# Limiting the upper words of 15 weight tiles in one ScalarE step, with a new early order on every engine

## The chip, the cores and the metric

The kernel runs on one core of one Trainium2 chip. The metric is the device time of one execution in microseconds; lower is better. The five engines of the core take part: TensorE (PE, with its weight loads as PEld), VectorE (DVE), ScalarE (ACT), GpSimd (POOL) and SyncE (SP), which here does nothing but issue DMAs.

## What is computed

Two layers, one after the other. The first is a gated linear attention over 4 batches, 8 heads, 768 positions and a head size of 48; the second takes its output as 3072 tokens of 384 values through a gated pair of matrix products with a hidden size of 2048.

```python
f = 1.0 / (1.0 + np.exp(-f_logit))
for t in range(S):
    state = f[:, :, t, :, None] * state + np.einsum('bhd,bhe->bhde', k[:, :, t], v[:, :, t])
    y[:, :, t] = np.einsum('bhd,bhde->bhe', q[:, :, t], state)
...
h = x @ w_in
relu6 = np.clip(h + 3.0, 0.0, 6.0)
g = h * relu6 / 6.0
return (g @ w_out).astype(np.float32)
```

The weights `w_in` and `w_out` come as float64 and are turned into float32 on the chip.

## The kernel before

**Units and groups.** The attention is cut into 24 units (`UNITS`): 6 blocks of 128 positions by 4 batches. Four units of one block make a group of 512 tokens, and each group then goes through 16 tiles `f` of 128 hidden columns: `mm1.f` (9 products of 128x128 with 128x512: high and low parts of weights and tokens, three of the four pairings), `relu.f` and `gh.f` on ACT, `g.f` and `gl.f` on DVE or POOL, `mm2.f` (9 products again). So 96 steps of each kind fill the program; `mm1.3` is tile 3 of group 0, `mm1.17` tile 1 of group 1. Tiles 0 to 2 of group 0 are computed in two halves of 256 tokens, `mm1a`/`mm2a` on units 0 and 1 and `mm1b`/`mm2b` on units 2 and 3, so that PE can begin when two units are done.

**One unit** `i` goes through: `load`, `loadq`, `loadv` (DMA of the gates, of q and k, of v), `gate` (sigmoid, ACT), `back` (a scan, DVE), `rend`, `end` (small), `kmul` (DVE or POOL), `fwd` (a scan, DVE), `qmul` (DVE or POOL); then on PE `tk` (transposes, copied out by `ktok` on ACT), `kv` (added up by `carry0` and `carry1`), `att` (masked by `mask` on DVE), `qs` and `av`; then `xh` (ACT) and `xl` write the high and the low part of the unit's output into `xts`. `xl` is a subtraction on DVE, or, where the order has `ym` for that unit, two products with minus the identity on PE and a copy on ACT. `hole` is two DMAs of 48 KB inside `xts`, which put rows where the next products expect them; `mm1a` waits for `hole.0` and `hole.1`, `mm1b` for `hole.2` and `hole.3`. In before, all of them are issued by SP.

**One weight tile** `f` goes through: `ld` (768 KB by DMA, issued by SP), the limit of the upper 16-bit words into `y`, `z` (ACT, L279: the lower words), `mid` (DVE, L286), `dif` (DVE, L291), `top` (DVE, L295: joins the two), `high` (ACT, L307: the high part as float32r) and `low` (DVE or POOL, L310: the rest). For tiles 0 to 2 half of `low` is split off: `wd` is a DMA, `lowi` the first half. The limit has two forms: for nine tiles (`ON_ACT`) ACT does two steps, `cy` (L267) and `lim` (L271), and for the other seven (0, 3, 7, 8, 13, 14, 15) DVE does one step, `lim` (L273).

**The order.** `ORDER` is a list of such tokens, made by a planner outside of the program. Each engine runs its own instructions in exactly the order in which the list names them (L844 to L849), and waits where an operand isn't there. `ON_POOL` names the steps that POOL does in DVE's place. `warm.N` and `tiny.N` are products of a blank tile that no one reads: they keep PE at work while it has nothing else. SP's list is in order too: a DMA whose buffer is still in use holds back all that stand behind it. DMAs share 8 semaphores in turn, so that one can also wait for the eighth before it.

Of the kernel before, what the change touches and what calls it, by code (L numbers as in the profile page):

```python
# [46 lines left out]
kmul.1 kmul.3 lowi.0 lowi.1 kmul.4 decay.4 kmul.5 qmul.5 decay.5 kmul.6 gl.4 decay.6 gl.5 qmul.6 kmul.7 low.10 low.11  # L47
gl.11 kmul.8 gl.14 qmul.9 lowo.0 kmul.9 decay.8 qmul.10 kmul.10 decay.9 decay.10 lowo.2 kmul.12 decay.12 qmul.13
qmul.14 qmul.15 kmul.15 decay.15 qmul.16 decay.16 qmul.17 qmul.18 decay.18 kmul.20 decay.19 decay.21 kmul.21 decay.22
kmul.22 qmul.23  # L50
# [6 lines left out]
end.0 warm.1 ktok.0 qmul.0 kv.0.0 back.1 load.2 att.0.2 carry0.0 ld.1 warm.1 loadq.2 rend.1 kmul.1 mask.0 fwd.1 tk.1.4
qs.0.0 lim.0 av.0 qmul.1 gate.2 warm.2 end.1 mid.0 ktok.1 load.3 back.2 loadq.3 carry1.0 kv.1.2 xh.0 loadv.2 z.0 ld.2
warm.9 rend.2 dif.0 loadv.3 fwd.2 cy.1 lim.1 top.0 ym.0 att.1.2 mid.1 gate.3 kmul.2 carry1.1 end.2 qmul.2 xl.0 tk.2.4
warm.2 carry0.1 mask.1 high.0 wd.0 qs.1.0 back.3 av.1 loadq.4 hole.0 att.2.2 xh.1 dif.1 kmul.3 warm.4 z.1 xl.1 load.4  # L60
mask.2 ktok.2 hole.1 lowi.0 cy.2 rend.3 top.1 tk.3.4 warm.2 ld.3 kv.2.2 ktok.3 lim.2 kv.3.0 fwd.3 carry0.2 z.2 warm.2
mid.2 qs.2.2 qmul.3 warm.2 carry1.3 dif.2 load.5 att.3.0 gate.4 ld.4 top.2 av.2 high.1 wd.1 mm1a.0.4 loadv.4 carry0.3
mask.3 lowi.1 end.3 carry1.2 loadq.5 xh.2 back.4 warm.1 high.2 ym.2 qs.3.0 relua.0 av.3 lowi.2 xl.2 kmul.4 lim.3
warm.1 xh.3 hole.2 mm1a.1.2 ga.0 end.4 xl.3 mm2a.0 relua.1 hole.3 decay.4 gate.5 ga.1 mid.3 z.3 rend.4 mm1a.2.1 dif.3
ld.5 fwd.4 wd.2 cy.4 ld.6 tk.4.4 mm2a.1 loadq.6 lim.4 qmul.4 top.3 ktok.4 ld.7 z.4 att.4.2 load.6 mid.4 ld.8 mm1b.0.4
back.5 relua.2 ld.9 high.3 ld.14 mm1b.1.0 ga.2 kmul.5 relub.0 rend.5 gb.0 cy.5 dif.4 kv.4.2 ld.10 mm1b.2.1 low.3 lim.5
loadv.5 top.4 mm2b.0 z.5 carry0.4 relub.1 mid.5 mm2a.2 mask.4 high.4 gb.1 cy.6 carry1.4 dif.5 mm2b.1 low.4 relub.2
lim.6 top.5 tk.5.0 mm1.3.3 z.6 mid.6 fwd.5 mm1.4.4 dif.6 qmul.5 relu.3 gb.2 end.5 high.5 g.3 decay.5 gate.6 low.5
att.5.2 ktok.5 mm2b.2 relu.4 back.6 top.6 qs.4.0 kmul.6 av.4 loadq.7 g.4 high.6 loadv.6 mask.5 loadv.7 mm1.5.4 gh.3
ld.12 lim.7 gh.4 load.7 low.6 ld.11 xh.4 gl.4 ld.15 gl.3 mm2.3 relu.5 rend.6 z.7 g.5 mid.7 z.8 lim.8 mm2.4 dif.7 gh.5  # L70
top.7 z.9 mid.8 mm1.6.2 high.7 dif.8 cy.9 low.7 end.6 top.8 kv.5.0 decay.6 relu.6 tk.6.4 lim.9 mm1.7.3 carry0.5 xl.4
gl.5 cy.10 mid.9 high.8 fwd.6 qs.5.0 relu.7 av.5 dif.9 qmul.6 mm2.5 xh.5 loadv.8 carry1.5 g.7 loadq.8 ktok.6 g.6 z.10
low.8 ym.5 lim.10 mm1.8.4 top.9 gate.7 gh.6 back.7 high.9 att.6.2 mid.10 gh.7 kv.6.0 kmul.7 gl.6 mm2.6 cy.11 rend.7
mask.6 lim.11 dif.10 z.11 low.9 tk.7.2 mm1.9.3 top.10 ktok.7 relu.8 fwd.7 high.10 end.7 relu.9 low.10 gl.7 mm2.7 g.8
carry0.6 gh.8 mm1.10.4 g.9 cy.12 carry1.6 qmul.7 xl.5 mid.11 load.9 gl.8 lim.12 mm2.8 ld.13 decay.7 hole.5 dif.11 gh.9
mid.12 z.12 dif.12 qs.6.2 top.11 att.7.0 loadq.9 top.12 av.6 high.11 load.8 kv.7.0 relu.10 gl.9 mm2.9 low.11 xh.6
carry0.7 mask.7 z.14 g.10 gate.9 qs.7.0 xl.6 z.13 lim.13 av.7 hole.6 mid.13 mm1.11.2 xh.7 lim.14 gh.10 loadv.9 dif.13
hole.4 mid.14 high.12 gl.10 mm2.10 top.13 relu.11 gate.8 g.11 low.12 gh.11 mm1.12.3 high.13 gl.11 carry1.7 xl.7 low.13
hole.7 mm1.13.4 dif.14 loadq.10 top.14 mm2.11 back.8 high.14 relu.12 low.14 kmul.8 z.15 mm1.14.1 lim.15 relu.13 g.12
g.13 mid.15 mm1.16.0 gh.13 dif.15 top.15 gl.13 tk.8.2 high.15 mm2.13 end.8 gh.12 low.15 relu.14 rend.8 gl.12 mm1.15.4  # L80
fwd.8 qmul.8 mm2.12 back.9 relu.15 load.10 relu.16 g.15 ktok.8 g.14 att.8.2 g.16 kv.8.2 gh.14 mm1.17.4 mask.8 gl.14
rend.9 gate.10 fwd.9 gh.15 mm2.14 gl.15 qmul.9 back.10 mm2.15 lowo.0 mm1.19.1 outs.0 outv.1 kmul.9 end.9 gh.16 outs.2
gl.16 decay.8 relu.17 mm1.18.0 od.2 rend.10 load.11 relu.19 g.17 od.0 carry0.8 fwd.10 mm2.16 relu.18 g.19 end.10
qmul.10 carry1.8 g.18 tk.9.3 kmul.10 load.12 lowo.1 mm1.20.4 loadv.10 ktok.9 od.1 gh.17 decay.9 gh.18 gl.17 gate.11
qs.8.0 back.11 att.9.2 decay.10 loadq.11 av.8 kv.9.2 gl.18 xh.8 mm2.17 gate.12 carry0.9 carry1.9 lowo.2 end.11 mask.9
mm1.21.2 gh.19 gl.19 xl.8 tk.10.3 relu.21 mm2.18 ktok.10 g.21 relu.20 rend.11 back.12 qs.9.0 gh.21 fwd.11 att.10.2
loadq.12 av.9 kv.10.0 qmul.11 mm2.19 g.20 load.13 loadv.11 carry0.10 gl.21 loadv.12 carry1.10 mm1.22.4 rend.12 fwd.12
kmul.12 mask.10 mm2.21 relu.22 g.22 decay.11 gh.22 kmul.11 mm1.23.3 gate.13 qmul.12 xh.9 back.13 load.14 hole.8
tk.11.4 relu.23 gl.22 mm2.22 ktok.11 xl.9 gh.20 g.23 hole.9 gl.20 qs.10.0 rend.13 att.11.2 gate.14 loadq.13 av.10
kv.11.0 loadv.13 tk.12.4 mm2.20 ktok.12 gh.23 end.12 gl.23 decay.12 mm1.24.4 mask.11 kmul.13 mm1.25.3 mm2.23 relu.25  # L90
relu.24 g.25 g.24 mm1.29.3 gh.24 gl.24 fwd.13 mm1.26.4 relu.29 gh.25 qmul.13 xh.10 gl.25 mm2.25 load.15 xl.10 relu.26
carry0.11 back.14 mm2.24 g.29 g.26 qs.11.0 gh.26 att.12.2 gl.26 av.11 kv.12.2 loadv.14 xh.11 carry1.11 mm2.26 mask.12
hole.10 gh.29 carry0.12 gate.15 carry1.12 loadq.14 rend.14 mm1.27.4 tk.13.2 relu.27 mm1.30.3 g.27 gl.29 xl.11 mm2.29
relu.30 hole.11 gh.27 g.30 end.13 kmul.14 mm1.28.1 gl.27 gh.30 ktok.13 gl.30 decay.13 back.15 tk.14.0 mm2.30 fwd.14
qmul.14 mm1.31.2 load.16 mm1.32.4 relu.31 relu.28 g.31 end.14 g.28 mm2.27 relu.32 ktok.14 qs.12.0 gh.28 att.13.2 gh.31
loadq.15 gl.28 av.12 kv.13.2 g.32 xh.12 mm2.28 decay.14 gate.16 mask.13 rend.15 carry0.13 carry1.13 fwd.15 mm1.33.4
# [870 lines left out]
```

## Time and profile before

| | |
|---|---|
| device time, median of 3 runs | 466.39 us (466.26 to 467.24) |
| span of the profiled execution | 464.7 us |
| PE busy | 453.4 us, 98% of the span |
| DVE, ACT, POOL busy | 291.0, 212.4, 64.3 us |
| DMA | 44.91 MB |

The profiled execution is told by its span, from its first to its last instruction; the page has no other time of it. The median of the timed runs is 1.7 us above the span, and that is what lies around it. PE's busy time counts the blank products too, and overlapping instructions once; the idle time of an engine is what stands "before" its instructions, with the event that ended it. Where two instructions of one engine follow each other without a wait, the second starts some 0.1 us before the first one's end, so that sums over a queue go by start to start.

### The profile page before, as it was taken

The numbers are of one execution on the slowest core, as the hardware profiler recorded it, in microseconds if no ns is written. First come the engines' busy times: TensorE is split into PE (matmuls) and PEld (weight loads), VectorE is DVE, ScalarE is ACT, GpSimd is POOL, SyncE is SP. The second block draws the span as 40 slices with busy tenths as digits, with TensorE's granted clock in tenths as the row PEclk, the third lists the DMA queues.
The fourth block names the chain that finished last, engine by engine and source line by source line (L and its number), as shares of the span: only waits on it lengthen the run. The fifth ranks groups of instructions, "written<-read, shape, count | busy, mean of one in ns | idle before, by whom it ended". The sixth has DMA issues, their size and how long they took to land.

```text
span 464.7 us, 11482 instructions
## 1 busy us (share of the span) xinstructions
PE 453.4 (98%) x4967; PEld 386.6 (83%) x4967; DVE 291.0 (63%) x455; ACT 212.4 (46%) x365; POOL 64.3 (14%) x65
## 2 busy tenths in 40 slices
...
GB/s 302 306 294 335 360 242 24 204 54 26 176 108 104 24 81 59 132 74 84 82 0 1 110 75 155 56 57 2 95 1 20 8 1 0 2 135 1 0 1 74
DMA packets 19113, 44.91 MB, mean 97 GB/s; under 512 B 2544, under 2 KB 8816, under 8 KB 19056
## 3 DMA queue, kind: packets, MB, share of 16 engines
...
q10 hardware_dynamic: 288, 0.26, 0.2%
q14 instruction: 16, 0.13, 0.1%
...
## 4 chain that ended last, share of the span: by engine, by line
PE 90%; DVE 3%; DMA 2%; ACT 2%; issue 1%; SPq 0%; POOL 0%; POOLq 0%
PE o L643 35%; PE pair L599 26%; PE single L599 11%; PE pair L514 3%; PE pair L444 2%; DMA v<-unit 2%; PE pair L531 2%; PE o L684 2%; PE idle L822 2%; PE pair L482 2%; PE pair L699 1%; PE single L699 1%; PE pair L463 1%; PE pair L665 1%; ACT w L279 1%
## 5 line engine op out<-in xcount | busy, mean ns | idle before, releaser
L643 PE MATMUL o<-gg,weight 128*128 128x512 f32 x705 | 165.7, 382 | 0.4 <-DVE gg L626 0.3
L643 PEld LDWEIGHTS o<-gg,weight 128*128 128x128 f32 x705 | 131.1, 189 | 19.8 <-DVE gg L626 1.6
L599 PE MATMUL pair<-xts,weight 128*128 128x512 f32 x576 | 133.1, 381 | 0.0
L599 PEld LDWEIGHTS pair<-xts,weight 128*128 128x128 f32 x576 | 107.6, 189 | 15.1 <-DVE tg L613 0.3
L626 DVE TENSOR_TENSOR gg<-tg,gg 128x512 fp32r<-128x512 f32 x75 | 56.0, 751 | 55.6 <-ACT gg L622 55.4
L622 ACT ACTIVATE gg<-tg 128x512 fp32r<-128x512 f32 x79 | 48.9, 626 | 65.7 <-PE o L643 51.3
L613 DVE SCALAR_TENSOR_TENSOR tg<-tg,pair 128x512 f32<-128x512 f32 x64 | 43.4, 683 | 55.8 <-ACT tg L609 55.6
L609 ACT ACTIVATE tg<-pair,half 128x512 f32<-128x512 f32 x64 | 43.5, 684 | 72.4 <-PE pair L599 69.1
L599 PE MATMUL single<-xts,weight 128*128 128x512 f32 x261 | 61.9, 382 | 0.0
L599 PEld LDWEIGHTS single<-xts,weight 128*128 128x128 f32 x261 | 48.5, 189 | 7.0 <-DVE tg L613 0.2
L609 ACT ACTIVATE tg<-single,half 128x512 f32<-128x512 f32 x29 | 19.9, 685 | 32.8 <-PE single L599 29.2
L376 DVE TENSOR_TENSOR_SCAN suffix<-gates,unit 112x516 f32<-112x516 f32 (+1 forms) x25 | 29.4, 1180 | 4.2 <-ACT gates L369 4.2
L400 DVE TENSOR_TENSOR_SCAN gates<-gates,rend 112x516 f32<-112x516 f32 x24 | 30.4, 1266 | 0.3
L389 POOL TENSOR_TENSOR qkf<-qkf,suffix 112x512 f32<-112x512 f32 x14 | 21.1, 1507 | 64.7 <-DVE suffix L376 22.2
L613 DVE SCALAR_TENSOR_TENSOR tg<-tg,single 128x512 f32<-128x512 f32 x29 | 19.8, 682 | 9.9 <-ACT tg L609 9.6
L408 POOL TENSOR_TENSOR decayed<-state,ends 112x192 f32<-112x192 f32 x13 | 10.6, 819 | 109.8 <-PE pair L514 65.8
L405 POOL TENSOR_TENSOR qkf<-qkf,gates 112x512 f32<-112x512 f32 x11 | 15.8, 1437 | 67.0 <-DVE gates L400 39.3
L550 ACT ACTIVATE xts<-pair 112x512 fp32r<-112x512 f32 x24 | 14.2, 594 | 23.6 <-PE pair L531 19.0
L451 DVE TENSOR_TENSOR a<-pair,causal 128x512 f32<-128x512 f32 x24 | 16.4, 683 | 8.2 <-PE pair L482 5.3
L643 PE MATMUL o<-xts,weight 128*128 128x512 f32 x84 | 20.3, 380 | 0.0
L563 DVE TENSOR_TENSOR xts<-pair,xts 112x512 fp32r<-112x512 f32 x21 | 14.4, 684 | 7.6 <-ACT xts L550 7.6
L626 DVE TENSOR_TENSOR xts<-tg,xts 128x512 fp32r<-128x512 f32 x14 | 9.5, 690 | 13.9 <-ACT xts L622 13.9
...
## 6 DMA issues: line engine op xcount, KB each, us to landing
...
```

The source lines that it names most:

```text
L376: nc.vector.tensor_tensor_scan(flat(sf[:, p])[:, ::-1], gt[:, columns(p)][:, ::-1], flat(unit[:, p])[:, ::-1], 0.0, op0=ALU.mult, op1=ALU.add,
L389: engine("kmul", i).tensor_tensor(parts_of(t, 1), parts_of(t, 1), split(sf[:, :, 1:C + 1]), op=ALU.mult)
L400: nc.vector.tensor_tensor_scan(past, past, flat(rend), 0.0, op0=ALU.mult, op1=ALU.add)
L405: engine("qmul", i).tensor_tensor(parts_of(t, 0), parts_of(t, 0), split(to), op=ALU.mult)
L451: nc.vector.tensor_tensor(d["a"].rearrange("r p e t -> r e p t"), d["at"], causal.unsqueeze(1).unsqueeze(1).broadcast_to([128, 2, NP, HC]) ...
L563: nc.vector.tensor_tensor(parts(1), d["y"][:PR], parts(0).bitcast(F32), op=ALU.subtract)
L599: nc.tensor.matmul(h, win(f, a, k), turned(g["xt"][:, k, :g["n"] // C, b]), start=i == 0, stop=i == 3 * KT - 1,)
L609: nc.scalar.activation(d["t"], d["h"], AF.Relu, bias=half, scale=1.0 / 6.0)
L613: nc.vector.scalar_tensor_tensor(d["t"], d["t"], 1.0, d["h"], op0=ALU.min, op1=ALU.mult)
L622: nc.scalar.activation(d["gg"][:, 0], d["t"], AF.Copy)
L626: engine("gl", g["first"] + f).tensor_tensor(d["gg"][:, 1], d["t"], d["gg"][:, 0].bitcast(F32), op=ALU.subtract)
L643: nc.tensor.matmul(g["o"][m], wout(f, a, m), halves_of(g[f]["gg"][:, b]), start=f == 0 and i == 0, stop=f == NF - 1 and i == 2, skip_group ...
```

## The change

Three things. The limit on ACT becomes one step: `y = Relu(TOP_LAST - x)`, written as an unsigned 16-bit number, takes the place of `cy` and `lim`, and the bounds of `mid` move with it. `ON_ACT` now holds 15 tiles, all but tile 2. And `ORDER`, `ON_POOL` and the names in `ON_ACT` are new: in the early part the order of every engine is another one, and `hole.0`, `hole.1` and `hole.3` are issued by ACT.

```diff
-    half, lowest, span = (const.tile([128, 1], F32, name=name) for name in ("half", "lowest", "span"))
+    half, topmost = (const.tile([128, 1], F32, name=name) for name in ("half", "topmost"))
...
-    nc.gpsimd.memset(lowest, float(32768 - TOP_ONE))
-    nc.gpsimd.memset(span, float(32768 - TOP_ONE + TOP_LAST))
+    nc.gpsimd.memset(topmost, float(TOP_LAST))
...
-    def conv_top(f):
-        nc.scalar.activation(joint(f, "y", U16), upper_of(f), AF.Relu, bias=lowest)
-
     def conv_limit(f):
         if on_scalar(f):
-            nc.scalar.activation(conv[f]["y"], conv[f]["y"], AF.Relu, bias=span, scale=-1.0)
+            nc.scalar.activation(joint(f, "y", U16), upper_of(f), AF.Relu, bias=topmost, scale=-1.0)
...
-            low, high = SPAN - LOWEST - TOP_ONE, SPAN - LOWEST + TOP_ONE
+            low, high = TOP_LAST - TOP_ONE, TOP_LAST + TOP_ONE
...
+            queue = nc.scalar if f"hole.{g['first'] // NF * B + j}" in ON_ACT else nc.sync
             for r in (0, 64):
-                nc.sync.dma_start(
+                queue.dma_start(
...
-lim.1 lim.2 lim.4 lim.5 lim.6 lim.9 lim.10 lim.11 lim.12
+lim.0 hole.0 hole.1 lim.1 lim.3 hole.3 lim.4 lim.5 lim.6 lim.7 lim.8 lim.9 lim.10 lim.11 lim.12 lim.13 lim.14 lim.15
```

How the orders move is seen at three places. The line numbers of after are 7 lower from the functions of a unit on.

**ACT, from the first unit's `xh` on.** In before: `xh.0`, `z.0`, the two limit steps of tile 1, `gate.3`, `carry1.1`, `end.2`, `xl.0`, `carry0.1`, `high.0`, `xh.1`.

```order
L550 ACTIVATE xts_117<-pair0_73 112x2x2x128
L279 ACTIVATE w0_302<-raw0_158 128x768
L267 ACTIVATE y1_320<-raw1_220,lowest_81 128x768
L271 ACTIVATE y1_320<-y1_320,span_82 128x768
L369 ACTIVATE gates1_78<-gates1_78 112x4x128
L502 ACTIVATE state1_111<-pair1_74 112x2x2x48
L395 ACTIVATE ends_116<-suffix0_77 112x4
L561 ACTIVATE xts_117<-pair0_73 112x2x2x128
L495 ACTIVATE middle1_106<-pair1_74 112x2x2x48
L307 ACTIVATE weight0_359<-w0_302 128x768
L550 ACTIVATE xts_117<-pair0_73 112x2x2x128
```

In after, from `xh.1` to `xh.2`: `xh.1`, `gate.3`, `ktok.2`, `xl.1`, `high.0`, the two DMAs of `hole.1`, `carry0.2`, `lim.1`, `carry1.2`, `z.1`, `xh.2`.

```order
L543 ACTIVATE xts_115<-pair1_74 112x2x2x128
L362 ACTIVATE gates1_78<-gates1_78 112x4x128
L463 ACTIVATE ktok2_380<-pair0_73 128x448
L554 ACTIVATE xts_115<-pair1_74 112x2x2x128
L300 ACTIVATE weight0_410<-w0_266 128x768
L562 DMA xts_115<-xts_115 16x3x256 x2
L488 ACTIVATE middle0_100<-pair0_73 112x2x2x48
L264 ACTIVATE y1_440<-raw1_310,topmost_81 128x768
L495 ACTIVATE state2_110<-pair0_73 112x2x2x48
L272 ACTIVATE w1_476<-raw1_310 128x768
L543 ACTIVATE xts_115<-pair1_74 112x2x2x128
```

Tile 1's limit has gone behind `xl.1` and takes one row where it took two, and the copies of `hole.1` stand between `high.0` and `carry0.2`.

**SP, from tile 0's weights on.** In before the gates of unit 2 come next, then tile 1's weights.

```order
L256 DMA raw0_158<-w 128x3072
L352 DMA gates0_76<-unit 128x517
L256 DMA raw1_220<-w 128x3072
L359 DMA qkf2_223<-unit 128x1024
L352 DMA gates1_78<-unit 128x517
L359 DMA qkf3_272<-unit 128x1024
L364 DMA v2_300<-unit 128x400
L256 DMA raw2_304<-w 128x3072
```

In after q, k and v of unit 2 stand ahead of its gates, and q and k of unit 4 and the gates of unit 3 ahead of tile 1's weights.

```order
L254 DMA raw0_131<-w 128x3072
L352 DMA qkf2_135<-unit 128x1024
L357 DMA v2_137<-unit 128x400
L345 DMA gates0_76<-unit 128x517
L352 DMA qkf4_232<-unit 128x1024
L345 DMA gates1_78<-unit 128x517
L254 DMA raw1_310<-w 128x3072
L352 DMA qkf3_343<-unit 128x1024
L254 DMA raw2_346<-w 128x3072
```

The gates of unit 2 have 712 KB more ahead of them, and tile 1's weights moved from the second place behind tile 0 to the sixth.

**ACT, around the second half of the tokens.** In before, between `xh.3` and `ktok.4` there are `end.4`, `relua.1`, `gate.5`, `z.3` and the two limit steps of tile 4.

```order
L550 ACTIVATE xts_117<-pair0_73 112x2x2x128
L395 ACTIVATE ends_116<-suffix0_77 112x4
L674 ACTIVATE th0_1_631<-pair1_74,half_80 128x256
L369 ACTIVATE gates1_78<-gates1_78 112x4x128
L279 ACTIVATE w3_640<-raw3_436 128x768
L267 ACTIVATE y4_657<-raw4_528,lowest_81 128x768
L271 ACTIVATE y4_657<-y4_657,span_82 128x768
L470 ACTIVATE ktok4_673<-single_75 128x448
```

In after `xh.3` is followed by `high.2`, `xl.3`, the copies of `hole.3`, `gate.5` and then `ktok.4`.

```order
L543 ACTIVATE xts_115<-pair0_73 112x2x2x128
L300 ACTIVATE weight2_628<-w2_486 128x768
L554 ACTIVATE xts_115<-pair0_73 112x2x2x128
L562 DMA xts_115<-xts_115 16x3x256 x2
L362 ACTIVATE gates1_78<-gates1_78 112x4x128
L463 ACTIVATE ktok4_665<-single_75 128x448
```

The copy of `ktok.4`, for which PE's `kv.4` waits, now stands behind the issue of `hole.3`.

PE's own list has 40 blank products of 512 columns in both; in before two of them stand behind `mm1a.0`, in after none. In before `kv.3` and `att.3` come ahead of `mm1a.0`, in after behind it. `ym` is done for units 0, 2 and 5 in before and for units 0 to 3 in after. POOL gives up `gl.4`, `gl.5`, `gl.11`, `low.11`, `lowo.0`, `lowo.2`, `decay.6` and `kmul.1`, `kmul.3`, `kmul.4` to DVE and takes `qmul.1`, `kmul.2`, `qmul.7`, `gl.15` and later five more `gl` from it.

## Rows read from the trace of the kernel before

**Rows 1.** Busy time of each engine by stage, us, with clock, DMA share, GB/s.
```profile
0.00:28.60 28.60, 23.09 (x532) 13.83 (x532) 23.37 (x36) 17.96 (x36) 6.32 (x21) 1.00 0.89 303
28.60:37.50 8.90, 8.35 (x100) 7.10 (x97) 8.08 (x13) 7.05 (x14) 2.29 (x3) 1.00 0.72 244
37.50:70.00 32.50, 32.28 (x397) 27.20 (x397) 31.34 (x50) 28.69 (x43) 10.96 (x8) 1.00 0.86 327
70.00:110.00 40.00, 39.53 (x478) 32.75 (x477) 39.25 (x61) 28.26 (x43) 9.00 (x5) 1.00 0.27 86
110.00:440.00 330.00, 329.91 (x3359) 287.68 (x3359) 181.00 (x286) 122.95 (x221) 35.76 (x29) 1.00 0.19 58
```

**Rows 2.** PE's groups by line, 0 to 28.6 us: busy us, mean ns, idle.
```profile
L822 PE MATMUL idle<-blank 128*128 128x512 bf16 x38 | 12.3, 456 | 1.1 <-DVE blank L219 1.1
```

**Rows 3.** PE in order of time: start us, busy us, what.
```profile
28.61 1.27 PE L665 MATMUL single<-xts,weight 128*128 128x256 f32 x9
...
36.09 1.47 PE L684 MATMUL o<-th,weight 128*128 128x256 f32 x6
37.49 0.69 PE L444 MATMUL pair<-qkf 48*64 48x64 f32 x32
38.12 1.27 PE L665 MATMUL single<-xts,weight 128*128 128x256 f32 x9
...
40.32 0.57 PE L482 MATMUL pair<-v,ktok 64*48 64x48 f32 x32
```

**Rows 4.** ACT in order of time from unit 2's gates on.
```profile
12.86 0.63 ACT L369 ACTIVATE gates<-gates 112x512 f32<-112x512 f32 x1 [3.75 <-DMA gates<-unit]
...
13.49 0.52 ACT L470 ACTIVATE ktok<-single 128x448 f32<-128x448 f32 x1
13.91 0.32 ACT L502 ACTIVATE state<-pair 112x192 f32<-112x192 f32 x1
14.12 0.60 ACT L550 ACTIVATE xts<-pair 112x512 fp32r<-112x512 f32 x1
14.60 0.91 ACT L279 ACTIVATE w<-raw 128x768 int32<-128x768 uint32 x1
15.41 0.99 ACT L267 ACTIVATE y<-raw,lowest 128x768 uint16<-128x768 int16 x1
16.49 0.94 ACT L271 ACTIVATE y<-y,span 128x768 uint16<-128x768 uint16 x1
```

**Rows 5.** DVE in order of time at the same place.
```profile
13.52 1.23 DVE L376 TENSOR_TENSOR_SCAN suffix<-gates,unit 112x516 f32<-112x516 f32 x1 [0.82 <-ACT gates L369]
...
19.11 0.69 DVE L451 TENSOR_TENSOR a<-pair,causal 128x512 f32<-128x512 f32 x1
```

**Rows 6.** Tile 1's weights alone: from issue (8.3 us) to landing.
```profile
DMA to landing us min/median/max: 6.3/6.3/6.3
```

**Rows 7.** SP's `hole` copies, 0 to 40 us: ns to issue one, us to landing.
```profile
L568 SPq DMA_DIRECT2D xts<-xts x8: 557/584/772, 20.4 to 34.2; - x8
...
DMA to landing us min/median/max: 2.4/4.2/5.4
```

**Rows 8.** The one early DMA on ACT's queue: KB, us to landing.
```profile
gates<-unit ACTq DMA_DIRECT2D x1, 129.0 KB, 2.8
```

**Rows 9.** Busy time of DVE's limit step (tile `raw`) by the stages of rows 1.
```profile
0.00:28.60 28.60, 0.53 (x1) 1.00 0.89 303
...
37.50:70.00 32.50, 1.44 (x2) 1.00 0.86 327
70.00:110.00 40.00, 2.96 (x3) 1.00 0.27 86
```

**Rows 10.** POOL and DVE in order of time around tile 3's limit.
```profile
30.87 1.27 POOL L389 TENSOR_TENSOR qkf<-qkf,suffix 112x512 f32<-112x512 f32 x1 [1.86 <-PE pair L514]
31.00 1.60 DVE L273 TENSOR_SCALAR y<-raw 128x768 int16<-128x768 int16 x1
```

**Rows 11.** DVE's `gl` steps, by line, 28.6 to 110 us: busy us, mean ns, idle.
```profile
L626 DVE TENSOR_TENSOR gg<-tg,gg 128x512 fp32r<-128x512 f32 x8 | 6.5, 808 | 0.0
```

178 lines of the change are left out of this document (88 added, 90 removed).

## The prediction, made before the kernel after was run

> **What bounds the kernel now.** I read the busy time by stage first. From 110 to 440 us PE is busy for 329.91 of 330 us, and from 37.5 to 110 us it is idle for 0.22 + 0.47 = 0.69 us [rows 1]. PE's real products are the same before and after (one unit more has `ym`, two small products), so behind 37.5 us no more than those 0.69 us can be won. The room is in front: up to 28.6 us, where `mm1a.0` starts [rows 3], PE is busy for 23.09 us [rows 1], of which 12.3 us are blank products that no one reads [rows 2]. So 5.5 + 12.3 = 17.8 of the first 28.6 us do nothing for the result. A change of the early order is worth what it brings `mm1a.0` and the steps behind it forward, if afterwards DVE, ACT and the DMAs keep up. That second condition is hard: from 37.5 to 110 us DVE is busy for 31.34 of 32.5 and 39.25 of 40 us [rows 1], since every weight tile passes through it.
>
> **The change part by part: the start.** I follow the new order with durations of the trace, start to start where a queue is full.
>
> Unit 2's gates: in before they land just ahead of 12.86 us, when ACT takes them [rows 4]. Now 712 KB of q, k and v stand ahead of them in SP's queue. In before 768 KB, tile 1's weights, stood right behind them and landed at 8.3 + 6.3 = 14.6 us [rows 6]; so the gates land between 12.9 (if the queue isn't what holds them) and 14.6 us. I take 14.4, because the amount of data is nearly that of the row. `back.2` follows as in before 0.66 us later [rows 4, 5], at 15.1 us, later by 1.5 us than now. Then `back.2` 1.23, `rend.2` some 0.1 and `mask.1` 0.69 [rows 5], `av.1` on PE about 0.69 like the 32 products of `att` [rows 3]: `xh.1` starts near 17.8 us.
>
> From there ACT's queue is full up to `xh.2`, and its rows give the time: `xh.1` 0.48, `gate.3` 0.6, `ktok.2` 0.42, `xl.1` 0.48 (a copy as wide as `xh`), `high.0` about 0.75, two DMA issues, `carry0.2` 0.21, one limit step 1.08, `carry1.2` 0.21, `z.1` 0.81, `xh.2` 0.6 [rows 4]. An issue of a `hole` copy takes SP 0.58 us [rows 7]; ACT's cost for one isn't in the trace, so its bounds are the fastest and the slowest of SP's, 0.56 and 0.77, and I take 0.58, so 1.17 for the two. The sum is 6.8 us: 24.6, and with `ym.2` of some 0.5 us `mm1a.0` starts at **25.1 us**, 3.5 us earlier than now.
>
> The single limit step is priced by L267, which reads the same words and writes the same: 1.08 us for what took 1.08 + 0.9 [rows 4]. For tile 0 ACT works where DVE did (0.53 us [rows 9]); in this stretch ACT gains one step and pays four DMA issues.
>
> **What the start gives back.** In before, `mm1a.0` to the end of `mm2a.1` takes 37.49 - 28.61 = 8.9 us [rows 3], with 0.55 us idle [rows 1] and two blank products of some 0.25 us: 7.8 us of work. The same list in after also holds `kv.3` (48 products against `kv.4`'s 32 in 0.57, so 0.85) and `att.3` (0.63 [rows 3]), which before had ahead of it: 9.3 us. Two waits come in. `kv.3` waits for `ktok.3`, which ACT reaches after `z.2` and `xl.2`, 0.4 us; `mm1a.1` waits for POOL's `lowi.1` 0.3 us. So 25.1 + 9.3 + 0.7 = 35.1 us. Next stands `kv.4`, and its `ktok.4` stands on ACT behind `hole.3`: PE ends `ym.3` near 32.3 us, then ACT does `high.2` and `xl.3` (1.2), two issues (1.17), `gate.5` (0.6) and `ktok.4` (0.53): 35.8 us. `kv.4` 0.57 and `att.4` 0.63 end at 37.0 us.
>
> There `mm1b.2` needs `hole.3`, whose second copy is issued near 34.1 us. Landing took 2.4 to 5.4 us, median 4.2, for SP's copies with weights ahead of them in the queue [rows 7], and 2.8 us for the one early DMA on ACT's queue [rows 8]. ACT's queue has nothing else in it, so I take 2.8: 36.9 us, in time. Before starts its first `mm1b` at 38.12 us [rows 3] and still owes `kv.4`, 0.57 us. So after is 38.12 + 0.57 - 37.0 = 1.7 us ahead.
>
> The Trainium skill ("DMA: Bandwidth & Descriptors", section "Issuing engines are not separate DMA queues") speaks against this part: all queues run on the same 16 DMA engines, and issuing from a second engine saves no more than issue time. By it the sum would take 4.2 us for the landing, and the lead would shrink to 0.4 us.
>
> **Does it last to 110 us?** DVE gives up six limit steps there, 1.60 + 1.44 + 2.96 = 6.0 us [rows 9, 10], and takes `gl.4`, `gl.5`, `gl.11` (0.81 each [rows 11]), `low.11` (half again as wide, 1.2) and `lowo.2` (0.5) from POOL, less `gl.15`. That is 6.0 - 3.3 = 2.7 us less work, which is more than the 1.7 us of lead that it has to follow. `kmul.4` against `qmul.7` and `xl.5` against `xl.3` cancel. ACT has nine times one step less, six times one more and two issues, and was idle there for 3.8 + 11.7 us [rows 1]. The new steps have a lower bound of nothing, where ACT waits anyway. Behind 110 us five more `gl` go to POOL while DVE is half idle [rows 1]: nothing.
>
> So the span becomes 464.7 - 1.7 = 463.0 us, and with the 1.7 us that lie around it the forecast is **464.7 us**.
>
> **The rivals.**
> - More is kept: the gates of unit 2 land at 12.9 and not at 14.4, and the waits of 0.7 us behind `mm1a.0` don't arise. ACT's order still has `gate.2` behind tile 0's limit, `z.0`, `xh.0` and `ktok.1`, so only some 0.9 of the 1.5 us come back. With the 0.69 us of idle time behind 37.5 us the gain reaches 1.7 + 0.9 + 0.7 + 0.7 = 4.0, so 462.4 us at best, and 463.3 in the middle.
> - The copies land no sooner from ACT. `hole.3` then lands at 34.1 + 4.2 = 38.3 and `mm1b.2` starts 1.3 us late; the gain is 0.4: 466.0 us. For it: until 70 us the DMAs are at a share of 0.86 [rows 1]. Against it: the row on ACT's queue.
> - DVE's relief isn't there. Alone its limit step takes 0.53 us [rows 9]; the long ones stood beside POOL, as the one of 1.60 us that ends 0.46 us after POOL's 30.87 + 1.27 [rows 10]. If that waiting passes to the neighbours, six steps free 3.2 us and not 6.0, DVE takes 3.3 back and can't follow: PE loses some 1.2 of the 1.7 us, 465.9 us.
> - Slower: ACT's issue of a copy costs more than SP's. ACT has just written what the copy reads, so the issue stands until that is written, and `carry0.2`, tile 1's limit and `xh.2`, then `gate.5` and `ktok.4`, stand behind. Two pairs lie on the path in series. At 2.0 us a pair in place of 1.17 the lead of 1.7 is gone; at 2.8 us it is 467.9 us. For it: no row shows ACT issuing between its copies. Against it: SP's slowest issue took 0.77 us [rows 7].
>
> The Trainium skill ("SBUF — State Buffer", section "SBUF: two separate sides") calls the ports that DVE and GpSimd share an exclusive lock, where the second one blocks for the whole instruction. The trace agrees, by that row of 1.60 us; by the rule the relief would be 3.2 us, the third rival's.
>
> **How the numbers follow.** Chances: the forecast 0.43 (its own range 463.9 to 465.6, from issue prices and the gates' landing), more kept 0.17, late copies 0.13, no relief 0.14, slower 0.13. The range that leaves out the slower case and the edge of the best is 462.5 to 466.6 us. A measurement of this kernel tells some 0.2% from no change, so 465.46 and 467.32 us are the borders. Faster: 0.41 of the forecast, 0.17, and 0.04 of the two cases near the border: 0.62. Slower: 0.12. Within: 0.26.
>
> **What would show it.** In the profile of after: `mm1a.0` near 25 us (24.2 to 26.5); ACT's limit near 1.1 us and its DMA issues near 0.6 us each; `back.2` near 15 us; landing of the copies from ACT's queue under 3 us; the first `mm1b` near 37 us; PE idle from there to 110 us for no more than 1 us, and 330 us behind it as full as now. It is wrong if `mm1a.0` starts after 27 us, if ACT stands idle around its DMA issues, or if PE waits for `low` or `high` of tiles 5 to 15 again and again, which would mean that DVE or the weights' DMAs, issued later in SP's new order, are the bound.

## The result, and the profile after

The kernel after takes **471.98 us** (median of 4 runs, 470.75 to 472.75) against 466.38 us for the kernel before: a ratio of 1.0115, 95% interval [1.0085, 1.0145]. It is slower by 5.6 us, where 464.7 us had been forecast. The profiled execution has a span of 471.0 us, against 464.7 us before. The executions of one kernel spread (the twelve of e1 below from 465.38 to 470.83 us), and a profile is one of them: the landings and waits below are those of one execution each, the ratios those of all.

The busy time by stage, with the columns of [rows 1] (stage, its length, PE, PEld, DVE, ACT and POOL busy, granted clock, DMA share, GB/s); the third stage of [rows 1] is cut in two here:

```profile
0.00:28.60 28.60, 23.38 (x465) 14.66 (x465) 22.71 (x33) 17.70 (x36) 6.57 (x20) 0.99 0.84 300
28.60:37.50 8.90, 8.81 (x162) 7.65 (x162) 6.15 (x13) 4.70 (x8) 0.30 (x1) 0.85 0.87 273
37.50:50.00 12.50, 8.15 (x126) 7.20 (x125) 9.24 (x17) 7.42 (x13) 0.97 (x2) 0.73 0.99 373
50.00:70.00 20.00, 20.00 (x215) 16.89 (x215) 16.69 (x28) 15.11 (x22) 4.78 (x4) 1.00 0.65 233
70.00:110.00 40.00, 40.00 (x453) 34.20 (x454) 38.27 (x64) 34.90 (x48) 6.23 (x4) 1.00 0.37 119
110.00:440.00 330.00, 329.91 (x3409) 286.78 (x3408) 182.76 (x287) 124.20 (x222) 37.16 (x31) 1.00 0.19 57
```

From 50 us on PE has no gap at all up to 110 us, and 329.91 of 330 us behind it, as before. All of the loss lies ahead of 50 us: PE is idle for 4.35 of the 12.5 us from 37.5 us on, and the granted clock is 0.85 and 0.73, where every stage of [rows 1] had 1.00. PE in order of time, the rows that answer to [rows 3], shows where (start, busy us, what; in brackets the idle time ahead of it and what ended it):

```profile
24.42 0.59 PE L547 MATMUL pair<-xts,minus 112*112 112x256 f32 x2
27.25 1.65 PE L659 MATMUL single<-xts,weight 128*128 128x256 f32 x9 [2.24 <-issue]
28.83 1.42 PE L475 MATMUL pair<-v,ktok 64*64 64x48 f32 x46
...
31.17 1.33 PE L659 MATMUL pair<-xts,weight 128*128 128x256 f32 x9
...
39.07 0.57 PE L475 MATMUL pair<-v,ktok 64*48 64x48 f32 x32 [0.90 <-ACT state L495]
39.46 0.66 PE L437 MATMUL pair<-qkf 48*64 48x64 f32 x32
43.57 2.26 PE L659 MATMUL pair<-xts,weight 128*128 128x256 f32 x9 [3.45 <-DMA xts<-xts]
45.63 2.13 PE L659 MATMUL single<-xts,weight 128*128 128x256 f32 x9
47.68 0.68 PE L507 MATMUL pair<-qkf,decayed 48*48 48x64 f32 x16
```

`ym.2`, the row of L547, is done when it was forecast. Then `mm1a.0` stands still for 2.24 us, and the first `mm1b` for 3.45 us, until a copy inside `xts` has landed. (The row of `mm1a.0` names no such end; it shows at the copies of `hole.1`, for which PE's weight load waited.) The first `mm1b` starts at 43.57 us, 5.45 us later than in before [rows 3]. Behind each of the two waits the products are slow: the first two `mm1b` take 2.06 and 2.05 us from start to start. The copies of `hole.1` and of `hole.3` in after (their issue, who waited for them, their landing):

```profile
L562 ACTq DMA_DIRECT2D xts<-xts x2: 563/564/564, 19.4 to 20.2; - x2
  PEld single L659: 2.4, 1
DMA to landing us min/median/max: 5.4/6.2/7.0
...
L562 ACTq DMA_DIRECT2D xts<-xts x2: 563/584/606, 36.5 to 37.1; - x2
  PE pair L659: 3.4, 1
DMA to landing us min/median/max: 5.8/6.1/6.4
```

The DMA issues of after from 14 to 45 us (out<-in, queue, count, KB each, median us from issue to landing):

```profile
raw<-w SPq DMA_DIRECT2D x10, 768.0 KB, 7.4
...
xts<-xts ACTq DMA_DIRECT2D x6, 48.0 KB, 6.0
xts<-xts SPq DMA_DIRECT2D x2, 48.0 KB, 2.4
```

The six copies on ACT's queue, which has nothing else in it, need 6.0 us to land. I had taken 2.8 us [rows 8]. The two of `hole.2`, which SP still issues, need 2.4 us. SP's issues show the difference from before. In before `ld.5` waits in SP's list until the copies of `hole.2` and `hole.3` are out:

```profile
31.16 3.59 SPq L568 DMA_DIRECT2D xts<-xts  x4
34.80 0.77 SPq L256 DMA_DIRECT2D raw<-w  x1
```

In after `ld.6` is out before ACT comes to `hole.3`:

```profile
35.62 0.73 SPq L254 DMA_DIRECT2D raw<-w  x1
```

**Two theories.** *A:* it does not matter which engine issues a copy. It lands when the loads issued ahead of it, on either queue, have landed; with ACT as issuer SP no longer waits for `xts` and runs ahead with loads of 768 KB, which then stand in front. *B:* ACT's queue as such is served late. A third question is how much of the loss is the clock rather than the waits, and a fourth whether the one-step limit costs something itself (*C*).

### The profile page after: what moved, and what is told of

Same layout as the page of the kernel before. It is cut to its first block, busy times and chain, and to the rows that moved or that the text cites. A ratio compares the mean times of both kernels' runs of the same rounds, so it can differ in the third digit from the quotient of the medians.

```text
span 471.0 us, 11466 instructions
## 1 busy us (share of the span) xinstructions
PE 456.8 (97%) x4967; PEld 391.1 (83%) x4967; DVE 286.5 (61%) x451; ACT 213.5 (45%) x363; POOL 56.0 (12%) x61
## 4 chain that ended last, share of the span: by engine, by line
PE 95%; DMA 1%; issue 1%; DVE 1%; ACT 1%; ACTq 0%
PE o L637 37%; PE pair L593 28%; PE single L593 10%; PE pair L507 3%; PE pair L524 3%; PE pair L475 2%; PE pair L437 2%; PE idle L816 2%; DMA xts<-xts 1%; PE pair L456 1%; PE o L678 1%; PE pair L693 1%; PE single L693 1%; PE single L659 1%; PE single L456 1%
## 5 line engine op out<-in xcount | busy, mean ns | idle before, releaser
L593 PE MATMUL pair<-xts,weight 128*128 128x512 f32 x612 | 141.5, 381 | 0.0
L593 PEld LDWEIGHTS pair<-xts,weight 128*128 128x128 f32 x612 | 114.4, 189 | 16.3 <-DVE tg L607 0.3
L607 DVE SCALAR_TENSOR_TENSOR tg<-tg,pair 128x512 f32<-128x512 f32 x68 | 46.3, 683 | 63.3 <-ACT tg L603 62.9
L620 DVE TENSOR_TENSOR gg<-tg,gg 128x512 fp32r<-128x512 f32 x72 | 52.8, 739 | 49.8 <-ACT gg L616 49.6
L603 ACT ACTIVATE tg<-pair,half 128x512 f32<-128x512 f32 x68 | 46.2, 685 | 69.9 <-PE pair L593 64.9
L593 PE MATMUL single<-xts,weight 128*128 128x512 f32 x225 | 53.3, 382 | 0.0
L593 PEld LDWEIGHTS single<-xts,weight 128*128 128x128 f32 x225 | 42.0, 189 | 5.9
L398 POOL TENSOR_TENSOR qkf<-qkf,gates 112x512 f32<-112x512 f32 x14 | 19.1, 1366 | 95.0 <-DVE gates L393 30.4
L607 DVE SCALAR_TENSOR_TENSOR tg<-tg,single 128x512 f32<-128x512 f32 x25 | 17.0, 678 | 8.5 <-ACT tg L603 8.3
L264 ACT ACTIVATE y<-raw,topmost 128x768 uint16<-128x768 int16 x15 | 17.4, 1160 | 2.3 <-DMA raw<-w 1.7
```

The source lines that it names most:

```text
L398: engine("qmul", i).tensor_tensor(parts_of(t, 0), parts_of(t, 0), split(to), op=ALU.mult)
L593: nc.tensor.matmul(h, win(f, a, k), turned(g["xt"][:, k, :g["n"] // C, b]), start=i == 0, stop=i == 3 * KT - 1,)
L603: nc.scalar.activation(d["t"], d["h"], AF.Relu, bias=half, scale=1.0 / 6.0)
L607: nc.vector.scalar_tensor_tensor(d["t"], d["t"], 1.0, d["h"], op0=ALU.min, op1=ALU.mult)
L620: engine("gl", g["first"] + f).tensor_tensor(d["gg"][:, 1], d["t"], d["gg"][:, 0].bitcast(F32), op=ALU.subtract)
```

## The experiments

### e1: after, with the copies issued by SP

```diff
-lim.0 hole.0 hole.1 lim.1 lim.3 hole.3 lim.4
+lim.0 lim.1 lim.3 lim.4
```

The three names leave `ON_ACT`; the written order stays.

> The kernel after, with the copies hole.0, hole.1 and hole.3 issued by SP again, at their places of the written order. Theory A (all queues share the DMA engines, and a copy lands when what was issued ahead of it, on either queue, has landed): the copies stand in SP's queue behind the loads and land no sooner than from ACT, 5 to 7 us after their issue, which now also waits for SP's turn; the first tile starts at 27 to 28 us, the first mm1b at 43 to 44.5 us, and the time is that of the kernel after within 1 us, 471 to 473 us. Theory B (ACT's queue is served worse than SP's): the copies land 2.4 to 4.2 us after their issue as hole.2 does, the first mm1b starts near 40 us, and the time falls to 466 to 468 us.

Measured 468.85 us, ratio 1.0038 [1.0012, 1.0063]: in between the two. The DMA issues of e1, first the stretch of `hole.1` (20.1 to 21.3 us), then that of `hole.3` (33.1 to 34.4 us):

```profile
xts<-xts SPq DMA_DIRECT2D x2, 48.0 KB, 4.0
...
xts<-xts SPq DMA_DIRECT2D x2, 48.0 KB, 6.8
```

`hole.3` needs 6.8 us from SP's queue, longer than the 6.1 us from ACT's in after, so theory B is out for it. `hole.1` is issued 0.6 us later than in after (20.1 and 20.8 against 19.4 and 20.2 us), and lands after 4.0 us in place of 6.2; SP can't issue `loadv.3` and `ld.3` ahead of its second copy any more (in after at 19.5 and 19.9 us). `mm1a.0` starts at 24.76 us without a wait. The number that I had expected under theory A for the first tile was wrong, since I had left out that SP's own waiting holds the loads back. What is left is one wait, 4.48 us ahead of the first `mm1b`:

```profile
24.76 1.17 PE L659 MATMUL single<-xts,weight 128*128 128x256 f32 x9
...
40.52 2.26 PE L659 MATMUL pair<-xts,weight 128*128 128x256 f32 x9 [4.48 <-DMA xts<-xts]
```

### e2: after, with blank products in the two waits

```diff
-ym.2 mm1a.0.4
+ym.2 warm.10 mm1a.0.4
...
-ld.9 mm1b.2.2
+ld.9 warm.15.2 mm1b.2.2
```

> The kernel after, with 10 blank products ahead of the first mm1a and 15 ahead of the first mm1b, on the PSUM buffers 4 and 2 that these take next, so that PE works while it waits; nothing else moves. Theory A: landings as in after (first mm1a near 27.2 us, first mm1b near 43.6 us), since the wait is for the copies; what goes is the time that the products behind the waits lose at a granted clock of 0.66 to 0.93, by their rows 0.5 us for the first mm1a, 0.8 for kv.3 and att.3 and 2 x 0.95 for the first two mm1b, some 3 us: 468 to 469.5 us. Rival (the loss is the waits alone and the slow products are slow for lack of data): the clock rises and the time stays at 471 to 472.5 us.

Measured 469.95 us, ratio 1.0066 [1.0042, 1.009]. PE of e2 in order of time:

```profile
39.66 3.41 PE L815 MATMUL pair<-blank 128*128 128x512 bf16 x15
42.72 1.35 PE L658 MATMUL pair<-xts,weight 128*128 128x256 f32 x9
43.91 1.17 PE L658 MATMUL single<-xts,weight 128*128 128x256 f32 x9
45.01 0.44 PE L506 MATMUL pair<-qkf,decayed 48*48 48x64 f32 x16
```

The copies land as late as in after (5.8 us for `hole.3`), but the granted clock is 1.00 in every stage up to 110 us, and the first two `mm1b` take 1.19 and 1.10 us where after has 2.06 and 2.05. So the slow products of after ran at the lower of TensorE's two levels (1.2 and not 2.4 GHz) because PE had stood idle ahead of them. In after the granted clock of these two products, from 43.57 to 47.68 us, is 0.50. The ratio falls by 0.0049, that is 2.3 us, with 0.5 to 4.1 us from the two intervals: of the 5.4 us that after loses by its ratio, some 2.3 are the clock, and 3.1 are the waits less what is given back. I had expected 3 us of clock, which lies within that.

### e3: after, with ld.3, ld.6 and loadv.5 held back

```diff
-hole.1 loadv.3 ld.3 mask.2 carry0.2 wd.0
+hole.1 loadv.3 mask.2 carry0.2 ld.3~carry0.2 wd.0
...
-hole.3 ld.6 qmul.4 loadv.5 mid.3 mm1a.2.3 gate.5 load.6
+hole.3 qmul.4 mid.3 mm1a.2.3 gate.5 ld.6~gate.5 loadv.5 load.6
```

(`~` holds a step until the last instruction of the one named has run.)

> The kernel after, with three groups of loads held back in SP's queue until the copies are issued: ld.3 waits for carry0.2 (behind hole.1 on ACT), ld.6 and loadv.5 behind it wait for gate.5 (behind hole.3 on ACT). Theory A: about 1 MB less stands ahead of hole.3 and some 400 KB less ahead of the second copy of hole.1, so hole.1 lands at 25 to 25.5 us in place of 27.16 and hole.3 at 39 to 40.5 us in place of 43.48; first mm1a near 25.5 us, first mm1b near 40 us, the granted clock of 40 to 50 us rises to 0.85 or more, and the time is 465 to 467.5 us. Theory B (ACT's queue is served worse than SP's whatever SP holds): landing stays 5 to 7 us and the time stays within 1 us of the kernel after, 471 to 473 us.

Measured 468.95 us, ratio 1.0031 [1.0004, 1.0058]: better than after, far from what theory A had promised, and `hole.3` still took 6.3 us to land. SP's issues show why I had held the wrong loads. `ld.4` and `ld.5` were issued at 31.2 and 31.6 us in place of 28.8 and 29.2, and these two, 1.5 MB, then stood ahead of `hole.3` just as `ld.6` had in after. The hold on `carry0.2` is not what made them late: it ended at 22.9 us, and SP then waited 3.8 us ahead of `hole.2` for unit 2's output, until 27.1 us (25.7 in after). In this execution, the longest of e3's twelve, unit 2's gates landed at 14.4 us, 1.5 us later than in after, the granted clock was 0.88 from 10 to 20 us, and ACT issued `hole.1` at 21.3 us; which of these made the output late is not shown. The run tells nothing between A and B.

### e4: before, with the limit in one step

```diff
-nc.scalar.activation(joint(f, "y", U16), upper_of(f), AF.Relu, bias=lowest)
...
-nc.scalar.activation(conv[f]["y"], conv[f]["y"], AF.Relu, bias=span, scale=-1.0)
+nc.scalar.activation(joint(f, "y", U16), upper_of(f), AF.Relu, bias=topmost, scale=-1.0)
```

The nine `cy` leave the order and the bounds of `mid` move, as in the change.

> The kernel before, in its own order, with the limit of its nine ACT tiles in one step in place of two (nine instructions of ACT less, 0.9 to 1.0 us each); nothing moves. Theory A (the loss comes from the copies' landing, the one step itself is a gain or nothing): within 0.2% of the kernel before, or up to 1 us faster, 465.4 to 466.6 us, with the limit step at 0.98 to 1.08 us of ACT. Rival C (the one step itself costs: its reading of every second word of the words that DVE or POOL write next): slower than the kernel before by 1 us or more.

Measured 466.54 us, ratio 1.0002 [0.9979, 1.0025]. Rival C, 1 us or more, falls but for the edge of the interval (1.2 us): by the median the step costs 0.1 us. Nor does it bring anything by itself that the measurement can tell, although ACT's busy time from 37.5 to 70 us goes from 28.69 [rows 1] to 23.75 us:

```profile
37.50:70.00 32.50, 31.02 (x367) 26.04 (x362) 30.94 (x49) 23.75 (x34) 11.30 (x8) 1.00 0.81 310
```

### e5: before, with three copies issued by ACT

```diff
-lim.1 lim.2 lim.4
+hole.0 hole.1 hole.3 lim.1 lim.2 lim.4
...
+queue = nc.scalar if f"hole.{g['first'] // NF * B + j}" in ON_ACT else nc.sync
...
-nc.sync.dma_start(
+queue.dma_start(
```

> The kernel before, in its own order with its two-step limits, with the copies hole.0, hole.1 and hole.3 issued by ScalarE: one part of the change alone. Theory A: SP no longer waits for the copies' tiles and issues the loads that stand behind them in its order at once (the gates of unit 3 and ld.3 behind hole.1, ld.5 behind hole.3), so these get ahead and the copies land 1 to 4 us later than in before (27.3 and 36.6 us); ACT pays 1.3 us for each pair; the first mm1b starts near 40 to 42 us in place of 38.12, and the time is 468 to 471 us. Forecast's own view (ACT's queue lands them in 2.8 us): within 1 us of before, 465.5 to 467.5 us.

Measured 473.16 us, ratio 1.0124 [1.0077, 1.017]. One part of the change alone, in the order of before, costs as much as the whole change. The DMA issues of e5 from 37.2 to 38.4 us, and PE's first `mm1b`:

```profile
raw<-w SPq DMA_DIRECT2D x1, 768.0 KB, 7.1
xts<-xts ACTq DMA_DIRECT2D x2, 48.0 KB, 6.5
```

```profile
44.53 1.24 PE L666 MATMUL single<-xts,weight 128*128 128x256 f32 x9 [2.74 <-DMA xts<-xts]
```

In before the same copies follow `hole.2` in SP's queue, which keeps SP from issuing the next weights; they land after 2.6 us, and `mm1b` starts at 38.12 us [rows 3]. In e5 SP issues `ld.5` at 35.1 and `ld.6` at 37.4 us, and the copies need 6.5 us. The sign and the place are as theory A says; the size is 2 us beyond its 471. The profile has a granted clock of 0.66 from 10 to 20 us as well, ahead of the first copy on ACT (21.1 us), where the edit moves nothing. Of the 6.4 us by which its first `mm1b` is late, 2.5 are there already at `mm1a.0` (31.11 against 28.61 us [rows 3]), which waits for no copy. So the profile has other losses than the copies, and how much of the median they are I can't say.

### e7: e1, with ld.5 behind hole.3

```diff
-ld.4 kmul.4 ld.5 qs.3.0
+ld.4 kmul.4 qs.3.0
...
-lowi.2 hole.3 ld.6
+lowi.2 hole.3 ld.5 ld.6
```

> The kernel e1 (after, the three copies issued by SP) with one load moved: ld.5, tile 5's weights of 768 KB, is issued behind hole.3 and not ahead of it, as the kernel before has it. Theory A (a copy lands when what was issued ahead of it has landed): hole.3 is issued near 32.5 to 33.5 us and lands near 36 to 37.5 us in place of 40.39, 3 to 4 us sooner, PE waits for it 1.5 us or less in place of 4.48, the products behind it run at full pace, and the time is 4 to 5.5 us under e1's, 463 to 465.5 us, faster than the kernel before. Rival (the DMA engines are full until 60 us, so what is late only moves: tile 5 or the next units wait instead): hole.3 lands early all the same, but the time stays within 1.5 us of e1's, 467.5 to 470 us.

Measured 465.77 us, ratio 0.9983 [0.9957, 1.0008]. The DMA issue of `hole.3` in e7 and the rows of PE:

```profile
xts<-xts SPq DMA_DIRECT2D x2, 48.0 KB, 2.6
```

```profile
26.06 1.24 PE L658 MATMUL single<-xts,weight 128*128 128x256 f32 x9 [1.38 <-DMA xts<-xts]
...
36.94 1.27 PE L658 MATMUL pair<-xts,weight 128*128 128x256 f32 x9 [0.40 <-DMA xts<-xts]
```

One load of 768 KB in another place takes the landing of `hole.3` from 6.8 to 2.6 us, the first `mm1b` from 40.52 to 36.94 us, and the ratio from 1.0038 to 0.9983, 2.6 us. The landing is as expected. The time is a little above the expected range, by medians 3.1 us under e1 and not 4 to 5.5, and in its profile the first `mm1a` waits 1.38 us for `hole.1`, where e1's does not, though the two orders are the same up to there.

### e8 and e9: after, copies on ACT, ld.5 held or only written later

```diff
-ld.4 kmul.4 ld.5 qs.3.0
+ld.4 kmul.4 qs.3.0
...
-hole.3 ld.6 qmul.4 loadv.5 mid.3 mm1a.2.3 gate.5 load.6
+hole.3 qmul.4 mid.3 mm1a.2.3 gate.5 ld.5~gate.5 ld.6 loadv.5 load.6
```

That is e8: `ld.5`, `ld.6` and `loadv.5` wait until `gate.5` has run, which stands behind `hole.3` on ACT. In e9 `ld.5` is written behind `hole.3`, and nothing is held.

> The kernel after, with the copies still issued by ACT, and ld.5, ld.6 and loadv.5 held back in SP's queue until gate.5 has run, which stands behind hole.3 on ACT. Theory A: hole.1 and the first mm1a as in after (27.2 us); hole.3 is issued near 36.5 us as there, but with only wd.2 ahead of it, and lands at 38.5 to 40 us in place of 43.48; the first mm1b starts near 39.5 us (kv.4 and att.4 end at 40.0), the clock of 40 to 50 us is back at 0.9 or more, and the time is 465.5 to 468 us. Theory B (ACT's queue itself lands late): landing stays near 6 us, first mm1b at 42.5 us or later, time 469.5 us or more.

> The kernel after, copies issued by ACT, with ld.5 written behind hole.3 as in e7 but nothing held. Theory A: since SP does not issue hole.3, the place in the written order holds nothing back; SP issues ld.5 as soon as wd.2 is out, near 35.6 us, so hole.3 (36.5 and 37.1 us) still stands behind it and ld.6, lands at 41 to 43.5 us, and the time is that of after within 1.5 us, 470 to 472.5 us. Rival (the written order is enough): hole.3 lands before 40 us and the time is that of e8.

e8 measured 465.13 us, ratio 0.9984 [0.9955, 1.0013]; e9, one execution, 471.04 us. The DMA issues around `hole.3` in e8 (34.5 to 35.8 us):

```profile
xts<-xts ACTq DMA_DIRECT2D x2, 48.0 KB, 2.6
```

and in e9 (36.1 to 37.4 us):

```profile
raw<-w SPq DMA_DIRECT2D x1, 768.0 KB, 8.6
xts<-xts ACTq DMA_DIRECT2D x2, 48.0 KB, 5.6
```

This settles A against B for `hole.3`. With ACT as issuer in both, the copy lands after 2.6 us with no weights in front, as from SP in e7 and in before, and after 5.6 us with them. e9 shows that a place in the written order holds nothing back when another engine issues: SP had issued `ld.5` at 35.3 us and begun with `ld.6` at 35.9, before ACT came to the copy at 36.1 us. Theory A is too strict in one point. The issue of `ld.6` went on until 37.4 us, beside that of the copies; they landed at 41.1 and 42.8 us, behind `ld.5` (41.0) but ahead of `ld.6` (44.5).

For `hole.1` less is shown. With `ld.2` in front and `ld.3` behind, it took 5.1 us in e7, 5.6 in e8 and 4.0 in e1, against 6.2 in after; so the part of `ld.3` is not clear of the spread, and `mm1a.0` still waits 1.41 us in e8. The first `mm1b` of e8 starts here:

```profile
37.20 0.57 PE L474 MATMUL pair<-v,ktok 64*48 64x48 f32 x32 [1.01 <-ACT state L494]
37.59 0.66 PE L436 MATMUL pair<-qkf 48*64 48x64 f32 x32
38.18 1.27 PE L658 MATMUL pair<-xts,weight 128*128 128x256 f32 x9
```

### e10 and e11: can the first wait go too?

e7 still waits 1.38 us for `hole.1`, with `ld.2` ahead of it. e10 puts `ld.2` behind `hole.1`, and the readers of tile 2 later; e11 puts it behind `loadv.3` too.

```diff
-carry1.1 ld.2 warm.2
+carry1.1 warm.2
...
-hole.1 loadv.3 ld.3
+hole.1 ld.2 loadv.3 ld.3
...
-mid.1 z.2 qmul.3
+mid.1 qmul.3
...
-xl.2 lim.2 end.3 ktok.3 hole.2 top.1 end.2 gate.4
+xl.2 end.3 ktok.3 hole.2 top.1 lim.2 end.2 gate.4 z.2
```

That is e10. Of e11 only what differs from it:

```diff
-hole.1 ld.2 loadv.3 ld.3
+hole.1 loadv.3 ld.2 ld.3
...
-top.1 lim.2 end.2 gate.4 z.2 kv.3.0 back.4 high.1 att.3.1 relua.0 wd.1
+top.1 end.2 gate.4 kv.3.0 back.4 lim.2 high.1 att.3.1 relua.0 z.2 wd.1
```

> The kernel e7 (copies issued by SP, ld.5 behind hole.3) with ld.2 too, 768 KB, issued behind hole.1 and not ahead of it; since tile 2's words then land near 26 us in place of 24.14, z.2 on ScalarE goes behind gate.4 and lim.2 on VectorE behind top.1, so that nothing queues behind them. Theory A: hole.1 lands at 23 to 24.7 us in place of 25.97, the wait of 1.38 us ahead of the first mm1a goes, and of this 0.5 to 1.2 us last to the first mm1b, which starts near 36 us: 464 to 465.5 us, 0.2 to 0.5% faster than the kernel before. Rival (the 1.4 us pass to the next wait, for POOL's share of lowi.1 ahead of mm1a.1, which stays at 28.8 us, or for tile 2's weights ahead of mm1a.2): the time is e7's, 465.3 to 466.3 us.

> The kernel e10 mended where it broke: loadv.3, for which kv.3 waited 2.46 us, is issued ahead of ld.2 again (hole.1, loadv.3, ld.2, ld.3), and the steps that read tile 2's words, lim.2 on VectorE and z.2 on ScalarE, stand behind back.4 and relua.0, so that high.1 no longer waits for them. Theory A (each load that is put behind the copy lands later by as much as the copy lands sooner, and the gain is what of it nobody waits for): hole.1 lands near 24.7 us, the first mm1a starts at 24.7 to 25 us in place of e7's 26.06, v.3 lands near 25.3 and kv.3 doesn't wait; ld.2 lands at 27.5 to 28.5 us; if tile 2's chain of limit, z, mid, dif, top and its split keeps up, 464 to 465.3 us. Rival (the chain of tile 2 is now last: mm1a.2, at 33 us in e7, waits 1 us or more for its weights): 465.5 to 468 us, no better than e7.

e10 measured 468.01 us, ratio 1.0034 [1.0006, 1.0063], worse than either theory had it. PE of e10:

```profile
24.85 1.24 PE L658 MATMUL single<-xts,weight 128*128 128x256 f32 x9 [0.32 <-DMA xts<-xts]
28.55 0.93 PE L474 MATMUL pair<-v,ktok 64*64 64x48 f32 x46 [2.46 <-DMA v<-unit]
```

`mm1a.0` did start 1.2 us sooner. But now `loadv.3` stood behind `ld.2`, and `kv.3`, the next on PE, waited 2.46 us for it; the clock fell to 0.67 from 30 to 40 us. I had looked at who waits for tile 2 and not at who waits for what stands behind tile 2.

e11 measured 466.03 us, ratio 0.9992 [0.9973, 1.0011]. That wait is gone, and the gain went to the next ones. The time lies in the rival's range, but the waits are not where it had them: `mm1a.2` doesn't wait for its weights, while `mm1a.1` waits for POOL's share of `lowi.1`, and `av.3` waits too:

```profile
29.39 0.60 PE L658 MATMUL pair<-xts,weight 128*128 128x256 f32 x3 [1.01 <-POOL weight L302]
32.43 0.31 PE L523 MATMUL pair<-a,v 64*48 64x64 f32 x2 [1.28 <-issue]
```

No kernel here beats the kernel before by more than a measurement can tell; e7 and e8 come nearest.

The kernels side by side, for `hole.3` (issue of its first copy; the last loads of 768 KB issued ahead of its second copy, and when; median us from issue to landing):

| kernel | issuer | issue | loads in front | landing | first `mm1b` | ratio |
|---|---|---|---|---|---|---|
| before | SP | 33.6 | `ld.4` 26.7 | 2.6 | 38.12 | 1 |
| after | ACT | 36.5 | `ld.6` 35.6 | 6.1 | 43.57 | 1.0115 |
| e1 | SP | 33.1 | `ld.4` 29.4, `ld.5` 29.8 | 6.8 | 40.52 | 1.0038 |
| e3 | ACT | 35.2 | `ld.4` 31.2, `ld.5` 31.6 | 6.3 | 42.16 | 1.0031 |
| e5 | ACT | 37.3 | `ld.5` 35.1, `ld.6` 37.4 | 6.5 | 44.53 | 1.0124 |
| e9 | ACT | 36.1 | `ld.5` 35.3, `ld.6` 35.9 | 5.6 | 42.99 | - |
| e7 | SP | 33.9 | `ld.4` 29.3 | 2.6 | 36.94 | 0.9983 |
| e8 | ACT | 34.5 | `ld.4` 30.0 | 2.6 | 38.18 | 0.9984 |
| e2 | ACT | 35.8 | `ld.6` 34.9 | 5.8 | 42.72 | 1.0066 |
| e10 | SP | 37.9 | `ld.4` 28.4 | 2.2 | 40.91 | 1.0034 |
| e11 | SP | 36.4 | `ld.4` 28.6 | 2.2 | 39.73 | 0.9992 |

An early landing is not all: e10 and e11 have the shortest landing, and what they gain by it goes to waits ahead of it.

## Why the prediction was wrong, point by point

**The start chain: right.** In e7 and e8, which have the same written order up to there, unit 2's gates landed at 14.2 us and `xh.1` started at 17.9 (forecast 14.4 and 17.8). In after's profile the gates landed at 12.9, the early end of the bounds. It brought little: `xh.1` started at 17.32 us, and `ym.2` at 24.42, where the forecast had ACT done at 24.6. So the premise of the rival "more is kept" came in this execution, without the 0.9 us that it was to give back. ACT's queue was not full, as I had it (it stood 0.72 us ahead of `carry0.2` and 0.60 ahead of `xh.2`), but its issues ran partly beside `high.0`, so that 6.9 us came out from `xh.1` to the end of `xh.2` where the forecast has 6.8. ACT's limit step took 1.01 us (forecast 1.08). The three pairs of issues took 1.32, 1.35 and 1.21 us on ACT (forecast 1.17), so the slower rival, dear issues, did not come: it needed 2.0 us.

**The landing of the copies: the step that failed.** I took 2.8 us because "ACT's queue has nothing else in it", from the one early DMA on that queue [rows 8], which had been issued when no weights were under way. Measured are 5.3 to 7.0 us. For `hole.1` I had not priced a landing at all: `mm1a.0` was to start when `ym.2` was done, at 25.1, and started at 27.25 us. For `hole.3` the second copy was to be issued at 34.1 and to land at 36.9; it was issued at 37.1 and landed 6.4 us later, at 43.5. Of the 6.6 us between, 3.6 are the landing, and 3.0 the later issue, of which the wait for `hole.1` handed on is some 2.2; the slow products behind it are the likely rest. I had also read [rows 7] too coarsely. Its eight copies aren't all such with loads in front: `hole.0` to `hole.2` took 4.1 to 5.4 us, and `hole.3`, the one that the forecast needed, 2.4 to 2.8: in before `ld.4` had landed, at 31.7 us, when its copies were issued, and `ld.5` stood behind them.

**What I overlooked in the change** is a side of "moved to ACT" that costs no engine time. In before, a `hole` in SP's list is a barrier: SP waits for `xh` and `xl`, and the weights behind it are not yet issued. Taken off that list, it holds back nothing, and the order that the planner writes between a copy on ACT and loads on SP is not kept by anything. The sentence of the Trainium skill that I had quoted against this part ("DMA: Bandwidth & Descriptors", "Issuing engines are not separate DMA queues") agrees with the runs: `hole.3` was no sooner from ACT in after (6.1 us) than from SP in e1 (6.8). I used it to set the landing at 4.2 us, the median of [rows 7], and not the upper end or beyond, although the new order has `ld.5` ahead of `hole.3`, where before has it behind, and nothing holds `ld.3` and `ld.6`, which it has behind `hole.1` and `hole.3`, until the copies are issued.

**The rival "late copies"** had the right place, the landing, with a third of its size: 1.3 us of wait, where 3.45 came, and no clock.

**The clock: not in the forecast at all.** With all rows at 1.00 [rows 1] I had no term for it. A wait of 2.2 or 3.45 us on PE with nothing in it costs more than its length here: 2.3 us for the two by e2 (0.5 to 4.1).

**The sum, from the rows.** The first `mm1b` is 5.45 us later than before; 0.57 of that is `kv.4`, which after has already done and before still owes [rows 3]; the two `mm1b` at the lower clock cost 2.06 + 2.05 - 1.19 - 1.10 = 1.8; and PE is full from there to 110 us, where before is idle for some 0.7 [rows 1]. That makes 5.45 - 0.57 + 1.8 - 0.7 = 6.0 us, against 6.3 between the two spans.

**The rest: right as far as it was tried.** In after DVE left no gap on PE from 50 us on, but PE came 5 us late, so that is no test of the rival "no relief". e8 is the better one: its first `mm1b` starts at 38.18 us, and PE is busy for 69.77 of the 70 us from 40 to 110 us (69.31 in before). DVE followed there, with a lead of only 0.5 us to follow. PE waited 0.90 us behind ACT's issues, where the forecast had 0.7; the profile names `carry1.3`, which stands right behind `ktok.4` on ACT.

**What the forecast was worth with its landing.** e8 is after with the landing that I had assumed for `hole.3`, 2.6 us in place of 6.1, though three loads are held back for it and `hole.1` still comes late (`mm1a.0` at 26.69 us, forecast 25.1). By the prediction's own count its first `mm1b` is 38.12 + 0.57 - 38.18 = 0.5 us ahead of before, where 1.7 were forecast. It has a ratio of 0.9984, 0.75 us faster than before, with an interval from 2.1 us faster to 0.6 slower; the forecast's 1.7 us lies in it. The part of the forecast that does not hang on the landing is thus not refuted, but too small to be shown.
